# The weight stream of the first MoE layer, moved within its quarters

## The chip, the cores and the metric

One core of a Trainium2 chip. The metric is the device time of one execution in microseconds, as the median of several runs. Engines: PE (TensorE, with PEld for its weight loads), DVE (VectorE), ACT (ScalarE), POOL (GpSimd), SP (SyncE), which here only issues transfers.

## What is computed

A chain of three parts on 1152 tokens of width 512, in float32:

- attention over 2 x 8 heads of 1152 keys of width 64, the queries pooled by two (576 per head), with a softmax;
- MoE 1: `h = x @ w_in` (512 x 2048), `g = elu(h)`, that is h where it is positive and exp(min(h, 0)) - 1 elsewhere, then `g @ w_out` (2048 x 512);
- MoE 2: a normalisation by the root mean square over the width, `silu(xn @ w_gate) * (xn @ w_val)` (512 x 1536 each), then a product with `w_out` (1536 x 512).

## The kernel before

**Products.** Every matrix product runs on a high and a low part of both operands (xh, xl, wh, wl, in fp32r): for each block of 128 rows of depth three matmuls, high x high (L216), low activation x high weight (L217), high activation x low weight (L218). `product` (L211) writes one bank of 128 x 384 from four such blocks: 12 matmuls, a full product; with `ks` of two blocks, 6 matmuls, a half product. The tokens are three chunks c of 384. Seven PSUM banks are handed out in turn by `bank`.

**MoE 1** runs in four quarters q (L832). A quarter has four blocks of w_in (first products, each followed by an elu) and four of w_out (second products, summed into x2). Weights are numbered in that order, so that quarter q uses weights 8q to 8q+3 for its first products and 8q+4 to 8q+7 for its second; weight 31 is the last of MoE 1. In quarters 1 to 3 the first products of two chunks are computed for a pair of weights with seven products instead of eight (class `Elu`, one object a pair, steps m1 to m7; 8 and 9 are the plain products of the third chunk), from sums of weight parts (`combine`, four POOL steps sf, then `round`: a cast and a subtraction) and sums of x parts (`sums_from_x`, made once in quarter 0). `run` (L810) takes the steps in an order written out by hand. MoE 2 works the same way with `Gate` from its third pair on; its first two pairs are plain products (`unit`), of which the first needs weights 32 and 34, the next 33 and 35.

**Second products.** In quarters 0 to 2 (L859 to L872) the order is: blocks 0 and 1 of the depth for output m = 0, then for m = 1, then blocks 2 and 3 for both, then full products for m = 2 and 3, each over chunks 2, 0, 1. Quarter 3 (L873) goes chunk by chunk, so that the normalisation of a chunk (class `Norm`: `square`, `sums`, `spread`, `scale`) can begin while the next is computed; before it ACT loads the table for Sqrt (L874).

**Elu** (L236): ACT takes Relu(-h) (L243) and Exp of its negative (L244), DVE joins them (L245) two products later, and three products later ACT casts the high part (L246) and POOL subtracts for the low part (L64, tiles gl, gel). Of seven products of a pair, one (in `both`, with `into`) has its sum in SBUF rather than in a bank.

**The weight stream** (class `Stream`). The weights arrive as 64-bit numbers of 512 KB a block and are turned into float32 by a generator, one instruction a step: two ACT steps (we, wm: L120, L122), three DVE steps (L131, L133, L136; the last frees the raw tile, and the load of a later weight is issued on SP), an ACT cast to the high part (wh, L183) and a POOL subtraction for the low part (wl, L64). With a pair's sums come six further steps. Every product is followed by `ws.step(wi, k)`, which emits up to k steps behind it; all engines work in order of emission, so k sets where in each engine's queue the stream stands. `step` stops at two gates: eight weights may be held from weight wi on (wi is raised as weights are done with), and sums of a pair wait for `limit`:

```python
                if self.done == len(self.srcs) or (self.alloc and self.at >= (i + WB if len(self.pools) > 1 else NE)):
                    return
                if self.pair is not None and self.pair >= self.limit:
                    return
```

If a product asks for a weight that is not there, `get` emits the missing steps on the spot.

Of the kernel before, what the change touches and what calls it, by code (L numbers as in the profile page):

```python
# [11 lines left out]
AF = mybir.ActivationFunctionType  # L12
ALU = mybir.AluOpType
# [26 lines left out]
def tile_kernel(ctx: ExitStack, tc: tile.TileContext, qd, kd, vd, w1d, w2d, wgd, wvd, wod, rgd, outd):  # L40
    nc = tc.nc
    V, G, T, PE, SP = nc.vector, nc.gpsimd, nc.scalar, nc.tensor, nc.sync
# [20 lines left out]
    def lo_pool(o, i, h):  # L63
        G.tensor_tensor(out=o, in0=i, in1=f(h), op=ALU.subtract)  # L64
# [146 lines left out]
    def product(out, w, a, first, last, ks=range(4)):  # L211

        wh, wl = w
        for k in ks:
            ah, al = a(k)
            PE.matmul(out, lhsT=wh[:, k, :], rhs=ah, start=first and k == 0, stop=False)  # L216
            PE.matmul(out, lhsT=wh[:, k, :], rhs=al, start=False, stop=False)  # L217
            PE.matmul(out, lhsT=wl[:, k, :], rhs=ah, start=False, stop=last and k == 3)  # L218

    def xchunk(c):  # L220
        return lambda k: (xh[:, k, cs(c)], xl[:, k, cs(c)])
# [3 lines left out]
    def defer(n, work):  # L225
        pending.append([n, work])

    def flush():
        for item in pending:
            item[0] -= 1  # L230
        due = [work for n, work in pending if n == 0]
        pending[:] = [item for item in pending if item[0]]
        for work in due:
            work()

    def elu(v, gh, gl, add=None, into=None):  # L236

        e = gp.tile([128, CH], F32, tag="eg", name="eg", bufs=6)
        if add is not None:
            ps, v = v, v if into is None else into  # L240
            V.tensor_tensor(out=v, in0=ps, in1=add, op=ALU.add)
        flush()
        T.activation(out=e, in_=v, func=AF.Relu, scale=-1.0)  # L243
        T.activation(out=e, in_=e, func=AF.Exp, scale=-1.0)  # L244
        defer(2, lambda: V.scalar_tensor_tensor(out=e, in0=e, scalar=-1.0, in1=v, op0=ALU.add, op1=ALU.max))  # L245
        defer(3, lambda: (T.copy(gh, e), lo_pool(gl, e, gh)))  # L246

# [192 lines left out]
    def emit_x(p, xs, a=0, b=QS):  # L440
# [7 lines left out]
        else:  # L448
# [5 lines left out]
    wi = 0  # L454
    ge = tuple(gep.tile([128, NE, CH], F32R, name=f"ge{n}", tag=f"ge{n}") for n in "hl")
    ws = Stream([w for q in range(4) for w in w_in[4 * q:4 * q + 4] + w_out[4 * q:4 * q + 4]]
                + [w[2 * i + n] for i in range(6) for w in (wgd, wvd) for n in range(2)] + [wod[i] for i in range(12)])
# [211 lines left out]
    for n in range(NE):  # L669
        elu(fb[:, n, 0:CH], ge[0][:, n], ge[1][:, n])  # L670
        ws.step(0, 3)
# [5 lines left out]
    def bank():  # L677

        nonlocal nbank
        n, nbank = nbank % 7, nbank + 1  # L680
        if n == 4 and len(psb) == 1:
            with tc.using_default_side("right"):
                psb.append(ctx.enter_context(tc.tile_pool(name="psC", bufs=3, space=PSUM)))
        return psb[n >= 4].tile([128, 512], F32, tag="b", name="b", bufs=3 if n >= 4 else 4)[:, 0:CH]
# [3 lines left out]
    def g_block(c, k):  # L688

        n = 4 * c + k  # L690
        return [t[:, n] for t in ge] if n < NE else [t[:, n - NE] for t in g_at]
# [100 lines left out]
    class Elu(Branch):  # L792
# [10 lines left out]
        def out(self, k, c, p, add=None, into=None):  # L803
            elu(p, *g_block(c, self.k + k), add, into)
# [5 lines left out]
    def run(order, limit, k=1):  # L810
        ws.limit = limit
        for br, m in order:
            br.m(m)
            ws.step(wi, 3 * k if m > 7 else k)
# [3 lines left out]
    wi = 0  # L818
    for i in range(4):
        w = ws.get(i)  # L820
        for c in range(3):
            if c == 0 and i < NE:
                continue
            ps = bank()
            product(ps, w, xchunk(c), True, True)
            elu(ps, *g_block(c, i))
            ws.step(wi, 3)
            if i > 1 and c == 2:
                next(sums_of_x)
        wi += 1  # L830

    for q in range(4):  # L832
        if q:
            old, b = None, Elu(2 * q)
            run([(b, k) for k in (1, 6, 5, 8, 7, 2, 9)], 2 * q + 2)
            old, b = b, Elu(2 * q + 1)
            run([(b, 1), (old, 4), (b, 8), (old, 3)], 2 * q + 2)
            run([(b, k) for k in (6, 5, 2, 7, 9, 4, 3)], 2 * q + 3)
            ws.limit = 2 * q + 4
            wi += 4  # L840

        def out1(c, m, b, then=None, ks=range(4)):
            product(b, ws.get(8 * q + 4 + m), lambda k: g_block(c, k), True, True, ks)
            flush()
            if then:
                then()
            if ks[-1] < 3:
                return
            x = x2[:, m, cs(c)]
            if q:  # L850
                V.tensor_tensor(out=x, in0=b, in1=x, op=ALU.add)
                if q == 3:
                    norms[c].square(m)
            elif c == 1:
                V.tensor_copy(x, b)
            else:
                T.copy(x, b)

        if q < 3:  # L859
            banks = {}  # L860
            for m, ks in ((0, (0, 1)), (1, (0, 1)), (0, (2, 3)), (1, (2, 3)), (2, range(4)), (3, range(4))):
                for c in (2, 0, 1):
                    if (m, c) not in banks:
                        banks[m, c] = bank()
                    out1(c, m, banks[m, c], None, ks)
                    if q == 0 and (m, ks[0]) != (1, 2):
                        next(sums_of_x, None)
                        if m == 1:
                            next(sums_of_x, None)
                    ws.step(wi, 5 if len(ks) > 2 else 3 if ks[0] == 0 else 2)  # L870
                if ks[-1] == 3:
                    wi += 1  # L872
        else:  # L873
            T.activation(out=dummy, in_=eps, func=AF.Sqrt)  # L874
            for c in range(3):
                if c == 0:
                    bs = [bank() for n in range(4)]
                    for n in range(4):
                        out1(c, n, bs[n], None, (0, 1))
                        ws.step(wi, 2)  # L880
                for n in range(4):
                    if c:
                        out1(c, n, bank(), norms[c - 1].sums if n == 1 else None)
                    else:
                        out1(c, n, bs[n], None, (2, 3))
                    if c and n == 2:
                        norms[c - 1].spread()

                    if c and n == 4 - c:
                        norms[c - 1].scale()  # L890
                    ws.step(wi, ((3, 3, 3, 0), (3, 3, 3, 0), (0, 6, 3, 3))[c][n])
            wi += 4
# [101 lines left out]
    b = Gate(2)  # L994
    run([(b, 1), (b, 8), (b, 9), (b, 2)], 2, 4, 2)
    run([(b, 6), (b, 5)], 2, 4)
    old, b = b, Gate(3)
    run([(b, 1), (old, 7)], 2, 4)
    for n in range(3, 11):
        if n > 3:  # L1000
            old, b = b, Gate(n)
# [7 lines left out]
    b = Gate(11)  # L1009
# [87 lines left out]
```

## Time and profile before

| | us |
|---|---|
| three runs | 686.48, 686.5, 687.26 (median 686.5) |
| the profiled execution | 689.09 |
| its span, first to last instruction | 687.3 |

The granted TensorE clock is 0.989 of full speed in the mean over the span; 58.66 MB are read from HBM, 89 GB/s. The profile is one execution. Busy times are sums over all stages; how much a stage can give is read from the waits and the clock inside it. MoE 1 lies between about 245 and 459 us of the span, MoE 2 behind it.

### The profile page before, as it was taken

The numbers are of one execution on the slowest core, as the hardware profiler recorded it, in microseconds if no ns is written. First come the engines' busy times: TensorE is split into PE (matmuls) and PEld (weight loads), VectorE is DVE, ScalarE is ACT, GpSimd is POOL, SyncE is SP. The second block draws the span as 40 slices with busy tenths as digits, with TensorE's granted clock in tenths as the row PEclk, the third lists the DMA queues.
The fourth block names the chain that finished last, engine by engine and source line by source line (L and its number), as shares of the span: only waits on it lengthen the run. The fifth ranks groups of instructions, "written<-read, shape, count | busy, mean of one in ns | idle before, by whom it ended". The sixth has DMA issues, their size and how long they took to land.

```text
span 687.3 us, 11390 instructions
## 1 busy us (share of the span) xinstructions
PE 667.6 (97%) x4149; PEld 657.1 (96%) x4149; DVE 502.9 (73%) x870; ACT 471.3 (69%) x924; POOL 447.2 (65%) x406
## 2 busy tenths in 40 slices
PE   8999999999999999899999998898999999999997
PEld 7999999999999999899999997897989999999997
DVE  7989899998988978837766757487777876776300
ACT  6888889888988959758659569345667555645300
POOL 5999889888988207966757756363998965323300
PEclk9999999999999999999999999899999999999999
DMA  5523333223331003321221321101233322204200
GB/s 172 183 87 120 123 118 104 87 88 127 124 110 65 1 1 112 105 92 62 93 93 62 123 93 62 61 32 61 93 123 125 129 85 92 93 1 137 86 35 34
DMA packets 21624, 61.75 MB, mean 90 GB/s; under 512 B 2752, under 2 KB 5056, under 8 KB 21568
## 3 DMA queue, kind: packets, MB, share of 16 engines
q1 hardware_dynamic: 21568, 61.03, 26.6%
q8 instruction: 32, 0.52, 0.3%
q14 instruction: 24, 0.20, 0.1%
HBM read 58.66 MB, written 2.36 MB: 89 GB/s over the span
## 4 chain that ended last, share of the span: by engine, by line
PE 80%; ACT 6%; POOL 5%; DVE 5%; issue 1%; DMA 0%; DVEq 0%; ACTq 0%; SPq 0%; POOLq 0%
PE b L743 15%; PE s L346 12%; PE o L390 11%; PE b L218 10%; PE b L217 10%; PE b L216 10%; PE t L364 10%; POOL gl L64 2%; POOL wl L64 2%; ACT eg L243 1%; ACT xh L728 1%; ACT eg L244 1%; DVE x L940 1%; ACT wh L183 1%; DVE wt L136 1%
## 5 line engine op out<-in xcount | busy, mean ns | idle before, releaser
L64 POOL TENSOR_TENSOR wl<-wt,wh 128x512 fp32r<-128x512 f32 x68 | 91.3, 1342 | 86.7 <-ACT wh L183 81.1
L70 DVE TENSOR_TENSOR ptl<-t,pth 128x384 fp32r<-128x384 f32 x216 | 106.7, 549 | 5.3 <-ACT pth L372 4.7
L350 DVE TENSOR_SCALAR_CACHE_REDUCE p<-s 128x1152 f32<-128x1152 f32 x72 | 97.4, 1353 | 14.8 <-PE s L346 14.2
L372 ACT CAST pth<-t 128x384 fp32r<-128x384 f32 x216 | 89.2, 487 | 21.9 <-PE t L364 21.1
L346 PE MATMUL s<-kd,qt 128*128 128x384 f32 x480 | 98.8, 343 | 2.1 <-DVE p L350 2.0
L355 ACT ACTIVATE p<-p,st 128x1152 f32<-128x1152 f32 x72 | 91.5, 1271 | 1.2 <-DVE p L350 0.9
L216 PE MATMUL b<-xh,wh 128*128 128x384 f32 x260 | 88.3, 340 | 1.8 <-ACT wh L183 1.8
L218 PE MATMUL b<-xh,wl 128*128 128x384 f32 x260 | 88.1, 339 | 0.7 <-POOL wl L64 0.7
L217 PE MATMUL b<-xl,wh 128*128 128x384 f32 x260 | 88.0, 338 | 0.0
L346 PEld LDWEIGHTS s<-kd,qt 128*128 128x128 f32 x480 | 81.2, 189 | 5.5 <-DVE p L350 3.1
L390 PE MATMUL o<-pth,vd 128*128 128x256 f32 (+1 forms) x288 | 84.4, 315 | 0.0
L364 PE MATMUL t<-ident,p 128*128 128x128 f32 x648 | 82.5, 273 | 0.0
L390 PE MATMUL o<-ptl,vd 128*128 128x256 f32 (+1 forms) x288 | 78.5, 295 | 0.0
L364 PEld LDWEIGHTS t<-ident,p 128*128 128x128 f32 x648 | 75.0, 141 | 2.0 <-ACT p L355 0.3
L120 ACT ACTIVATE we<-wr 128x512 uint32<-128x512 uint32 x68 | 45.4, 668 | 39.1 <-DMA wr<-in_w_dram 17.1
L131 DVE TENSOR_SCALAR wm<-wm 128x512 f32<-128x512 f32 x63 | 43.7, 693 | 21.1 <-ACT wm L122 21.1
L122 ACT ACTIVATE wm<-wr 128x512 f32<-128x512 f32 x63 | 39.6, 629 | 25.3 <-DVE wt L136 25.1
L390 PEld LDWEIGHTS o<-pth,vd 128*128 128x128 f32 x288 | 54.4, 189 | 0.3
L390 PEld LDWEIGHTS o<-ptl,vd 128*128 128x128 f32 x288 | 54.4, 189 | 0.0
L64 POOL TENSOR_TENSOR gl<-eg,gh 128x384 fp32r<-128x384 f32 x36 | 39.1, 1103 | 18.8 <-ACT gh L246 18.7
L217 PE MATMUL b<-gl,wh 128*128 128x384 f32 x144 | 49.2, 342 | 2.1 <-POOL gl L64 2.0
L216 PEld LDWEIGHTS b<-xh,wh 128*128 128x128 f32 x260 | 49.2, 189 | 2.1 <-ACT wh L183 2.1
(195 smaller groups left out, 1771.8 us busy)
## 6 DMA issues: line engine op xcount, KB each, us to landing
wr<-in_w_dram SPq DMA_DIRECT2D x32, 512.0 KB, 3.2
rawq<-in_q_dram SPq DMA_DIRECT2D x15, 576.0 KB, 4.5
rawk<-in_k_dram SPq DMA_DIRECT2D x28, 288.0 KB, 2.8
wr<-in_wg_dram SPq DMA_DIRECT2D x12, 512.0 KB, 3.2
wr<-in_wv_dram SPq DMA_DIRECT2D x12, 512.0 KB, 3.2
wr<-in_wo_dram SPq DMA_DIRECT2D x12, 512.0 KB, 3.3
rawv<-in_v_dram SPq DMA_DIRECT2D x16, 288.0 KB, 2.8
out_dram<-o SPq DMA_DIRECT2D x12, 192.0 KB, 1.8
```

Of the source, the lines that this page charges most:

```text
L64: G.tensor_tensor(out=o, in0=i, in1=f(h), op=ALU.subtract)
L70: V.tensor_tensor(out=o, in0=i, in1=f(h), op=ALU.subtract)
L216: PE.matmul(out, lhsT=wh[:, k, :], rhs=ah, start=first and k == 0, stop=False)
L217: PE.matmul(out, lhsT=wh[:, k, :], rhs=al, start=False, stop=False)
L218: PE.matmul(out, lhsT=wl[:, k, :], rhs=ah, start=False, stop=last and k == 3)
L346: PE.matmul(s[:, m, 0:384], lhsT=a, rhs=b[:, 384 * m:384 * m + 384], start=n == 0, stop=n == len(parts) - 1)
L350: V.tensor_scalar(out=pt, in0=s[:, :, 0:384], scalar1=-0.0625, scalar2=None, op0=ALU.mult, op1=ALU.min, accum_out=st[p][:, 0, TILES[i][4], :])
L355: T.activation(out=pt, in_=pt, func=AF.Exp, scale=-1.0, bias=st[p][:, 0, TILES[i][4], :], accum_out=st[p][:, 1, TILES[i][4], :])
L364: PE.transpose(ps[:, k, :], src[:, 128 * b:128 * b + 128], ident)
L372: T.copy(oh, re(ps))
L390: PE.matmul(self.o[:, 0:self.N], lhsT=v[:, b, :], rhs=(pth, ptl)[u][:, g["buf"], b, g["c0"]:320], start=self.n == 0, stop=self.n == 17)
L743: PE.matmul(out, lhsT=a[x][:, k, :], rhs=b[y][:, k, :], start=first and (k, x, y) == (0, 0, 0), stop=last and (k, x, y) == (1, 1, 0), skip ...
```

## The change

- The first products of quarter 0 emit two stream steps instead of three behind those of weights 2 and 3.
- The second products of quarters 0 to 2 emit 0, 3, 4, 4, 7, 7 steps behind each product of their six groups, instead of 3, 3, 2, 2, 5, 5.
- In quarters 1 to 3, wi is raised by two when the first pair is done and by two more at the end, instead of by four at the end.
- The elu of a block whose sum is in SBUF takes min(h, 0) on DVE and Exp of it, instead of Relu(-h) on ACT and Exp of its negative.
- In quarter 0 the results of all three chunks are copied out by DVE, instead of two of them by ACT.
- The sums of x get two calls behind some products that had one.

```diff
         flush()
-        T.activation(out=e, in_=v, func=AF.Relu, scale=-1.0)
-        T.activation(out=e, in_=e, func=AF.Exp, scale=-1.0)
+        if into is not None:
+            V.tensor_scalar(out=e, in0=v, scalar1=0.0, scalar2=None, op0=ALU.min)
+        else:
+            T.activation(out=e, in_=v, func=AF.Relu, scale=-1.0)
+        T.activation(out=e, in_=e, func=AF.Exp, scale=-1.0 if into is None else 1.0)
...
             elu(ps, *g_block(c, i))
-            ws.step(wi, 3)
+            ws.step(wi, 3 if i < 2 else 2)
...
             run([(b, 1), (old, 4), (b, 8), (old, 3)], 2 * q + 2)
+            wi += 2
             run([(b, k) for k in (6, 5, 2, 7, 9, 4, 3)], 2 * q + 3)
             ws.limit = 2 * q + 4
-            wi += 4
+            wi += 2
...
-            elif c == 1:
+            else:
                 V.tensor_copy(x, b)
-            else:
-                T.copy(x, b)
...
                     if q == 0 and (m, ks[0]) != (1, 2):
                         next(sums_of_x, None)
-                        if m == 1:
+                        if (m, ks[0]) != (0, 0):
                             next(sums_of_x, None)
-                    ws.step(wi, 5 if len(ks) > 2 else 3 if ks[0] == 0 else 2)
+                    ws.step(wi, 7 if len(ks) > 2 else 4 if ks[0] else 3 * m)
```

## Rows read from the trace of the kernel before

**Rows 1.** The page, part 1: busy us, share of the span, instructions.

```profile
PE 667.6 (97%) x4149; PEld 657.1 (96%) x4149; DVE 502.9 (73%) x870; ACT 471.3 (69%) x924; POOL 447.2 (65%) x406
```

**Rows 2.** Waits of PE: engine, line, releaser: us in total, times, longest.

```profile
PE b L216 <- ACT wh L183: 5.3, 2, 3.5
PE b L218 <- POOL wl L64: 2.8, 2, 2.1
...
PE b L217 <- POOL gl L64: 2.0, 1, 2.0
```

**Rows 3.** Stretches of 5 us: busy us (instructions) by engine, granted clock, DMA share, GB/s.

```profile
275.00:280.00 5.00, 5.00 (x31) 5.00 (x30) 4.97 (x6) 4.13 (x8) 5.00 (x5) 1.00 0.09 34
285.00:290.00 5.00, 5.00 (x25) 5.00 (x25) 2.28 (x4) 2.90 (x8) 4.46 (x3) 0.81 0.45 151
315.00:320.00 5.00, 5.00 (x31) 5.00 (x30) 2.84 (x6) 4.91 (x12) 5.00 (x5) 1.00 0.20 79
500.00:505.00 5.00, 3.71 (x21) 3.22 (x20) 3.21 (x7) 4.10 (x9) 5.00 (x4) 1.00 0.31 108
```

**Rows 4.** Timeline of POOL around 273 to 283 us: start, length, operation.

```profile
273.56 4.41 POOL L64 TENSOR_TENSOR gl<-eg,gh 128x384 fp32r<-128x384 f32 x3
277.92 2.03 POOL L64 TENSOR_TENSOR wl<-wt,wh 128x512 fp32r<-128x512 f32 x1
279.90 2.70 POOL L64 TENSOR_TENSOR gl<-eg,gh 128x384 fp32r<-128x384 f32 x2
```

**Rows 5.** Timeline of PE around 280 us: start, length, operation.

```profile
279.28 0.33 PE L216 MATMUL b<-gh,wh 128*128 128x384 f32 x1
...
280.32 0.34 PE L216 MATMUL b<-gh,wh 128*128 128x384 f32 x1
...
286.93 0.34 PE L217 MATMUL b<-gl,wh 128*128 128x384 f32 x1
```

**Rows 6.** Timeline of PE around 426 to 437 us.

```profile
426.02 0.33 PE L218 MATMUL b<-geh,wl 128*128 128x384 f32 x1
...
437.20 0.34 PE L217 MATMUL b<-gl,wh 128*128 128x384 f32 x1
```

**Rows 7.** Timeline of ACT around 426 to 430 us.

```profile
425.89 1.28 ACT L874 ACT_TABLE_LOAD   x1
...
427.29 0.49 ACT L246 CAST gh<-eg 128x384 fp32r<-128x384 f32 x1
...
428.80 0.49 ACT L246 CAST gh<-eg 128x384 fp32r<-128x384 f32 x1
429.20 0.61 ACT L183 CAST wh<-wt 128x512 fp32r<-128x512 f32 x1
```

**Rows 8.** Timeline of POOL around 429 to 433 us.

```profile
429.38 1.96 POOL L64 TENSOR_TENSOR gl<-eg,gh 128x384 fp32r<-128x384 f32 x2 [0.51 <-ACT gh L246]
431.29 1.27 POOL L64 TENSOR_TENSOR wl<-wt,wh 128x512 fp32r<-128x512 f32 x1
```

**Rows 9.** Timeline of PE around 466 to 478 us.

```profile
466.08 0.83 PE L711 MATMUL b<-ones,sq 128*128 128x1 f32 x6 [0.74 <-DVE sq L706]
...
470.84 0.34 PE L218 MATMUL b<-xh,wl 128*128 128x384 f32 x1
...
477.47 0.79 PE L721 MATMUL b<-ident,rr 128*128 128x128 f32 x3
```

**Rows 10.** Timeline of DVE around 462 to 472 us.

```profile
462.13 0.69 DVE L131 TENSOR_SCALAR wm<-wm 128x512 f32<-128x512 f32 x1
...
465.94 5.62 DVE L940 TENSOR_TENSOR x<-x 128x768 f32<-128x768 f32 x4
```

**Rows 11.** The page, part 6: DMA issues, KB each, us from issue to landing.

```profile
wr<-in_w_dram SPq DMA_DIRECT2D x32, 512.0 KB, 3.2
```

**Rows 12.** Timeline of ACT around 354 us.

```profile
353.83 0.47 ACT L755 COPY m<-b 128x384 f32<-128x384 f32 x1
```

**Rows 13.** The chain that ended last, in order of time: start, length, what.

```profile
351.23 3.15 PE b L743 x18
```

## The prediction

> **What bounds the kernel now.** I read the page first. TensorE (PE) is busy for 97% of the span [rows 1], so this change can give back only what PE loses by waiting and by running slowly after a wait. The list of waits by engine says where: the longest are for a weight's high part from ACT and its low part from POOL, and one of 2.0 us for the low part of an activation [rows 2]. The stretches of 5 us place them. Between the listed places PE is busy throughout; ACT is the fullest helper in the first products of a quarter (4.91 of 5 us), without holding PE up [rows 3]. After each long wait the granted clock falls: 0.81 over the 5 us behind the 2.0 us wait [rows 3]. So a wait costs its length and slow matmuls behind it. Quarters 1 and 2 can hardly gain; what can are four places: the start of quarter 0's second products, the start of quarter 3's, the change from MoE 1 to MoE 2, and the first combined products of MoE 2.
>
> **What moves.** I counted on the code which stream step is emitted behind which product. Second products of quarters 0 to 2: before 3x(3+3+2+2+5+5) = 60 steps each, after 3x(0+3+4+4+7+7) = 75; none behind the first three half products, more behind the full ones. Quarter 0's first products with weights 2 and 3 lose five steps in all. The first products' own 26 steps stay, but the stream may now take the buffers of a pair two weights earlier. By the count, the low part of weight 31 (last of MoE 1) is emitted in quarter 3's first products, before it was behind the third half product of its second ones; weight 35's (the last that MoE 2's first units need) moves from behind MoE 2's first unit into quarter 3. Every weight carries the same steps as before: 5 on ACT and DVE, a cast, a POOL subtraction, one DMA on SP's queue. None is added; each load is still issued when DVE has released its buffer, and SP has no other transfer queued in this part. The extra calls for the sums of x in quarter 0 change nothing: ten are left, and the tenth is reached behind the same product.
>
> **Place A, second products of quarter 0.** POOL runs three activation subtractions in 4.41 us, weight 6's in 2.03, two more in 2.70, and the last of these is what PE waits for [rows 4]. At full speed a matmul starts every 0.173 us (six between 279.28 and 280.32); from 280.32 to 286.93 are 16, 2.8 us of work in 6.6, so 3.8 us are lost [rows 5]: 2.0 in the wait [rows 2], 1.8 to the slow clock behind it. The change emits weight 6's subtraction five products later. Its 2.03 us come off POOL ahead of the last one, which then ends by 280.57, against 280.49 when PE asks. ACT and DVE lose at least three and one stream steps there, so its inputs come sooner too. I take 3.8; the low end is 2.0, POOL's own time alone, with the slow clock kept.
>
> **Place B, second products of quarter 3.** From 426.19 (the end of 426.02's slot) to 437.20 PE issues 16 matmuls, 2.8 us of work in 11.0: 8.2 us lost, to weight 31 and the slow clock after it [rows 6]. Afterwards weight 31 is ready. What is late next? The activation of this half product's last block. ACT first loads the Sqrt table (425.89), casts one block at 427.29, and casts the needed one at 428.80 [rows 7]. In the new order weight 33's cast (0.53, from 429.20 to 429.73) stands between, instead of two steps of weight 32, so the needed cast ends near 428.6. POOL takes one subtraction to about 428.9, weight 33's (1.27) to 430.1, then the needed one (0.98) to 431.1 [rows 8]. PE asks at 426.19 + 10 x 0.173 = 427.9. That leaves 3.2 us, and as in A 1.8 of slow clock: 5.0 instead of 8.2. I take 3.2. The ends are 0 (another wait as long) and 8.2 (none).
>
> **Place C, change to MoE 2.** From 470.84 to 477.47 PE makes 13 steps, 2.3 us in 6.6: 4.4 lost to weight 35 and the clock; the sum of squares waits another 0.7 [rows 9]. Weight 35's cast sat behind casts that wait for DVE's four subtractions (5.62 us from 465.94), and these sat behind three stream steps from 462.13 on, 0.69 each [rows 10]. The gate of eight weights keeps the stream out of the last third of quarter 3's products, so these 2.1 us leave DVE's queue, and weight 35 is ready long before. I take 4.4 + 0.7 = 5.1. The low end is 2.5, the two waits for weight 35 alone (5.3 - 3.5 and 2.8 - 2.1 [rows 2]), with a slow clock kept behind another wait: the scale of the last third, late for a PE that arrives sooner.
>
> **Place D, first combined products of MoE 2.** PE idles 1.29 of 5 us at 500 [rows 3]. The stream is a step or two further by emission order, but PE arrives some 5 us sooner after the change of MoE. I take half, 0.6, between 1.3 and a loss of 1.
>
> **The moved steps.** Six Relu steps leave ACT, each near its 0.49 us step of [rows 7], and six minimum steps join DVE. No row shows one; the ends are nothing and 0.69 us, the 128x512 step of [rows 10], and with POOL in its way 0.69 + 1.47 = 2.2: POOL's 128x384 subtraction takes 1.47 us (4.41/3) while DVE is busy 4.97 of 5 us [rows 3, 4], but 0.98 at another place [rows 8]. The Exp behind each now waits for DVE, and behind that Exp on ACT stand the Relu and casts of the next blocks. I take nothing for all six: their results are needed only in the next half products, and ACT, the fuller engine, loses more than it waits [rows 3]. Without that cover they cost up to 6 x 2.2 = 13 us. The Trainium skill (SBUF — State Buffer, section "Who interferes with whom") speaks against such a move: tensor_scalar between SBUF tiles can enter a two-port mode, in which DVE and GpSimd exclude each other for a whole instruction. By that rule each step would stand behind a POOL subtraction or hold one up; the two POOL durations above agree with it, and the sum would be near 0 instead of 12.7 only if all six reached PE.
>
> The eight result copies of quarter 0 that move from ACT to DVE cost under 0.69 each beside products of 2.1 us, and seven banks rotate; I cost them at nothing. If DVE were late with one, PE would wait for its bank.
>
> **New pressure.** Seven steps behind a 2.1 us product is a weight per 2.7 us. With two raw buffers two weights need: a load 3.2 [rows 11], two ACT steps near 0.53 each [rows 7], three DVE steps of 0.69 [rows 10]: 6.3, so 3.2 for each, and with queueing some 3.3. The stream therefore falls behind, and at the end of quarter 1's second products ACT reaches the next copy late. Before, that copy ran at 353.83, although its product ended near 351.23 + 3.15/3 + 0.2 = 352.5 [rows 12, 13]. Carried forward weight by weight I get about 354.7, then two DVE steps to 356.0; PE needs them at 351.23 + 3.15 + 2.1 = 356.5 [rows 13]. I cost this at nothing; the cover is half a microsecond thick in quarter 1, one in quarter 0. If it goes, a start costs up to 2 us and 1.8 of slow clock.
>
> **Sum.** 3.8 + 3.2 + 5.1 + 0.6 = 12.7 us. The profiled execution took 689.09 with a span of 687.3, 1.8 us around it; it should go to 676.4 with a span of 674.6. The median of the runs is 686.5, 2.6 below the profiled one: 673.8. About 0.2% (1.4 us) is what a measurement here tells from no change.
>
> **Rivals.** (1) Place B vanishes whole, if ACT's queue is clear and the needed subtraction slips ahead: 5.0 more, 668.8. For it speaks that ACT has fewer steps in quarter 3; against it that the table load and the chain in front of it don't move [rows 7]. Chance 0.12. (2) The wait changes place: quarters 1 to 3 each start with a stall of up to 2 us plus slow clock, together 3 to 10 us: 677 to 684. For it speaks the half microsecond of cover; against it that in the first products the stream stands still at its gate more often, which leaves ACT room. 0.20. (3) The stream does not get ahead, because gate or raw buffers stop it: only A is gained, 682.7. For it: one more buffer gate hit in quarter 2's last two products by the count. 0.07. (4) Slower: ACT is held by late loads at all three starts, past the 356.5 of [rows 13]. It decides from 12.7/3 = 4.2 us a start, so 2.4 of stall and 1.8 of clock; that is ACT some 3 us later than I carried it, near 358. At 3.5 of stall each: 686.5 - 12.7 + 3 x 5.3 = 689.7. 0.04. (5) DVE's minimum steps and POOL's subtractions exclude each other, and all six reach PE at their full bound of 13 us: 686.8, no change. Against it: no listed wait of PE is for such a step [rows 2]. 0.02. That is the rule of the Trainium skill named above, taken to its end.
>
> **Numbers.** The forecast, 0.55, spans 670 to 677. The range takes in rival 1, most of rival 2 and the ends of B and C: 668.0 to 681.0, leaving out rivals 3 to 5 and the end of 2, about 0.2. Faster by over 0.2%: 0.55 + 0.12 + 0.20 + 0.07 = 0.94; same 0.02; slower 0.04.
>
> **What would show it.** Right: no wait of PE for a low activation part near 280, no clock under full there; no wait for a weight's parts at quarter 3's start, instead one near 3 us for an activation's low part; none for weight 35; first products of quarters 1 to 3 without PE waits. Wrong: PE waiting for a copy's reader or a bank at those starts, ACT's raw weight step waiting longer for loads and PE behind it, or a weight still the releaser at quarter 3.

## The result and the profile after

The changed kernel took 679.56 us (median of four runs, 679.0 to 680.05), the kernel before 686.88 beside it (four runs, 686.48 to 689.01): a ratio of 0.9887, interval 0.9865 to 0.9909. Measured again (e8, below) the ratio was 0.9881 (0.9863 to 0.9899). So it is faster, by 7.3 us and not by the 12.7 of the sum; the time lies inside the range of 668 to 681, near its slow end, and outside the forecast's 670 to 677. The profiled execution took 680.05 with a span of 678.2.

Part 1 of the page of the changed kernel, busy us by engine; it answers to [rows 1]:

```profile
PE 663.7 (98%) x4149; PEld 654.5 (96%) x4149; DVE 511.3 (75%) x884; ACT 465.2 (69%) x910; POOL 446.0 (66%) x406
```

PE's busy time fell by 3.9 us with the same 4149 matmuls: I read that as fewer slow matmuls; the waits that went come on top. DVE has 14 instructions more and ACT 14 fewer: six minimum steps and eight copies.

The waits of PE in the changed kernel (engine, line, releaser: us in total, times, longest), which answer to [rows 2]:

```profile
PE b L217 <- POOL gl L64: 2.5, 2, 1.9
PE b L746 <- DVE u L781: 2.1, 1, 2.1
...
PE b L216 <- ACT gh L249: 1.4, 1, 1.4
...
PE b L746 <- POOL tsl L64: 0.7, 1, 0.7
```

No weight is waited for any more: 5.3 and 2.8 us of [rows 2] are gone. In their place stand an activation's high and low part, and a wait of 2.1 us for DVE's `u` (L781: the sum that DVE reads off step m6's bank; step m7 goes on in that bank and waits for it) that the kernel before had nowhere at this length. The stretches place them (columns: stretch, length, busy us and instructions of PE, PEld, DVE, ACT, POOL, granted clock, DMA share, GB/s); they answer to [rows 3]:

```profile
285.00:290.00 5.00, 5.00 (x31) 5.00 (x30) 4.47 (x8) 2.22 (x4) 3.44 (x4) 1.00 0.59 195
300.00:305.00 5.00, 4.29 (x25) 3.97 (x24) 3.95 (x6) 2.44 (x5) 4.92 (x6) 1.00 0.51 187
305.00:310.00 5.00, 2.94 (x17) 2.62 (x16) 2.04 (x4) 3.96 (x7) 4.46 (x5) 1.00 0.30 106
...
430.00:435.00 5.00, 3.63 (x11) 3.63 (x12) 1.22 (x3) 1.58 (x4) 3.16 (x4) 0.50 0.26 97
```

Behind place A the clock is full now (1.00 where it was 0.81). The new hole is at 305 to 310, where quarter 1's first pair begins, and place B still loses clock (0.50).

**Where the time went, place by place.** The start of one and the same matmul in two profiles tells how far ahead the changed kernel is there. Taken against a second execution of the kernel before (experiment e0, span 684.6), in us:

| the matmul stands | before, again | after | ahead of before |
|---|---|---|---|
| last of the attention | 239.81 | 240.38 | -0.57 |
| in place A, past the wait | 281.90 | 281.13 | 0.77 |
| quarter 1, step m7, past the wait for u | 305.38 | 307.81 | -2.43 |
| quarter 3's second products, past place B | 436.15 | 436.66 | -0.51 |
| MoE 2, past place C | 474.60 | 469.60 | 5.00 |
| MoE 2, first combined products (D) | 501.24 | 494.77 | 6.47 |

The differences between successive rows are the gains: A 1.3, start of quarter 1 -3.2, the stretch to the end of place B 1.9 (of it 1.6 at B), C 5.5, D 1.5; together 7.0, near the medians' 7.3, after 0.6 lost ahead of the change. Against the profile that the prediction read (span 687.3), with A taken behind its slow matmuls, the same list is A 2.9, start of quarter 1 -3.2, B 2.4, C 5.2, D 1.6.

**The new wait.** The timeline of ACT in the changed kernel (start, length, operation; in brackets idle time and releaser):

```profile
302.98 0.60 ACT L183 CAST wh<-wt 128x512 fp32r<-128x512 f32 x1
305.74 1.04 ACT L170 CAST tsh<-sf 128x1024 fp32r<-128x1024 f32 x1 [2.16 <-POOL sf L162]
306.69 0.47 ACT L758 COPY m<-b 128x384 f32<-128x384 f32 x1
```

of POOL:

```profile
299.17 2.38 POOL L64 TENSOR_TENSOR tsl<-sf,tsh 128x1024 fp32r<-128x1024 f32 x1
301.51 1.29 POOL L64 TENSOR_TENSOR wl<-wt,wh 128x512 fp32r<-128x512 f32 x1
302.76 0.74 POOL L156 TENSOR_TENSOR sf<-wt 128x256 f32<-128x256 f32 x1
...
304.96 0.74 POOL L162 TENSOR_TENSOR sf<-wt,sf 128x256 f32<-128x256 f32 x1
305.66 1.27 POOL L64 TENSOR_TENSOR wl<-wt,wh 128x512 fp32r<-128x512 f32 x1
```

and of PE:

```profile
307.81 0.45 PE L746 MATMUL b<-tsh 128*128 128x384 f32 x1 [2.06 <-DVE u L781]
```

The copy of m1 (L758) could run by 303 us (in e4, below, it does at 302.83), but it stands on ACT behind the cast of a pair's sums (L170), which is emitted by the stream behind the last second product. That cast waits 2.16 us for POOL, and POOL is the late one: a pair of weights costs it two subtractions of 1.3, four sums of 0.74 and one subtraction of 2.38, some 7.9 us, and from 293.7 on one follows the other. That run itself began late: POOL stood idle for 2.98 us before it, until a cast of ACT whose raw weight ACT had awaited for 2.56 us (to 291.94). So the load, which the prediction did count, has a share in it. Copy 306.69, DVE's u 307.19, PE 307.81: one chain.

### The profile page after: what moved, and what is told of

Its sections match the earlier page's. It is cut to its first block, busy times and chain, and to the rows that moved or that the text cites. A ratio compares the mean times of both kernels' runs of the same rounds, so it can differ in the third digit from the quotient of the medians.

```text
span 678.2 us, 11378 instructions
## 1 busy us (share of the span) xinstructions
PE 663.7 (98%) x4149; PEld 654.5 (96%) x4149; DVE 511.3 (75%) x884; ACT 465.2 (69%) x910; POOL 446.0 (66%) x406
## 4 chain that ended last, share of the span: by engine, by line
PE 47%; POOL 4%; ACT 2%; DVE 2%; issue 1%; DMA 1%; DVEq 0%; ACTq 0%; POOLq 0%; SPq 0%
PE b L746 15%; PE b L217 11%; PE b L216 11%; PE b L218 10%; POOL wl L64 1%; POOL tsl L64 1%; DMA wr<-in_w_dram 1%; POOL gl L64 0%; POOL sf L162 0%; POOL sf L158 0%; POOL sf L156 0%; ACT xh L731 0%; POOL xl L64 0%; ACT we L120 0%; ACT wm L122 0%
## 5 line engine op out<-in xcount | busy, mean ns | idle before, releaser
L70 DVE TENSOR_TENSOR ptl<-t,pth 128x384 fp32r<-128x384 f32 x216 | 106.7, 549 | 4.9 <-ACT pth L375 4.4
L216 PE MATMUL b<-gh,wh 128*128 128x384 f32 x144 | 49.0, 341 | 1.4 <-ACT gh L249 1.4
```

What stands on the lines that cost most here:

```text
L70: V.tensor_tensor(out=o, in0=i, in1=f(h), op=ALU.subtract)
```

## Experiments

The theory: the 3 us at quarter 1's start are lost because the stream's cast waits for POOL with the copy of m1 queued behind it; the rest of the error is the size of the slow clock at A and B. Rivals: the copies moved to DVE, the moved Relu steps, or the stream's pace as such, which would give a wait back elsewhere. Ratios are to the kernel before, run beside each on the same chip.

**e0: the kernel before once more.**

> The kernel before once more, for a second profile. Its first profile gives 9.0 us to the change (offsets of the same matmuls), the medians only 7.3. If the first profile was a long execution, this one's span is nearer to 684.7 (median 686.5 less 1.8 around the span), and one of the places A to D loses less than 3.8, 8.2, 5.1 and 1.3 us, most likely by a shorter stretch at the lower clock. If instead the profile itself lengthens the kernel, the span is 687 again and the places lose the same.

It took 686.4, span 684.6, against 689.09 and 687.3 of the profile that was read. The waits are the same, `gl` too. Its stretch behind place A:

```profile
285.00:290.00 5.00, 5.00 (x30) 5.00 (x29) 3.69 (x7) 3.07 (x8) 5.00 (x5) 1.00 0.49 164
```

and its wait there:

```profile
PE b L217 <- POOL gl L64: 2.0, 1, 2.0
```

The same wait of 2.0 us, and a clock of 1.00 where [rows 3] has 0.81. Of the two profiled executions only the first has the slow clock at A; by the starts of the same matmuls it cost 1.6 us there, most of the 2.6 by which that execution stood above the median.

**e1: three steps instead of seven behind the last second product of quarter 0**, so that the pair's cast is emitted behind the copy.

```diff
-                    ws.step(wi, 7 if len(ks) > 2 else 4 if ks[0] else 3 * m)
+                    ws.step(wi, 3 if (q, m, c) == (0, 3, 1) else 7 if len(ks) > 2 else 4 if ks[0] else 3 * m)
```

> The changed kernel, with three stream steps instead of seven behind the very last second product of quarter 0, so that the cast of pair 3's sums is emitted behind the copy of quarter 1's first product and not ahead of it. Theory (queue on ACT behind POOL): PE waited 2.06 us at 307.8 because that copy stood on ACT behind the cast, which waited for POOL's fourth sum step. That wait goes, the copy runs near 303.5, the 0.70 us wait at 301.6 stays: 679.6 - 2.1 = 677.5. Rival (the copies moved to DVE make DVE late): DVE has the same work, the wait stays, 679.6. Rival (late loads set the pace): the wait shrinks by less than 0.5 us, above 679.0.

678.2 us, ratio 0.9862 (0.9836 to 0.9887). ACT at quarter 1's start, with the cast behind the copy:

```profile
302.93 0.47 ACT L758 COPY m<-b 128x384 f32<-128x384 f32 x1
305.19 1.05 ACT L170 CAST tsh<-sf 128x1024 fp32r<-128x1024 f32 x1 [1.78 <-POOL sf L162]
```

ACT at quarter 3's start, the copy behind a late load:

```profile
401.85 0.66 ACT L120 ACTIVATE we<-wr 128x512 uint32<-128x512 uint32 x1 [3.39 <-DMA wr<-in_wg_dram]
...
402.96 0.48 ACT L758 COPY m<-b 128x384 f32<-128x384 f32 x1
```

The cast still waits for POOL, but nothing hangs on it: PE no longer waits at quarter 1's start. It waits 1.1 us at quarter 2's and 0.8 at quarter 3's instead, where ACT's first steps of a weight stand ahead of the copy and wait for a load (2.41 us at 352.22, and the row above). So the theory holds at the first place, and much of what it returns is given back at the other two as long as their order stays: the time alone does not tell e1 (expected at 677.5) from the changed kernel.

**e4: no steps behind the last second product of quarters 0 to 2**, seven steps later, behind m5 of the next quarter.

```diff
-            run([(b, k) for k in (1, 6, 5, 8, 7, 2, 9)], 2 * q + 2)
+            run([(b, k) for k in (1, 6, 5)], 2 * q + 2)
+            ws.step(wi, 7)
+            run([(b, k) for k in (8, 7, 2, 9)], 2 * q + 2)
...
-                    ws.step(wi, 7 if len(ks) > 2 else 4 if ks[0] else 3 * m)
+                    ws.step(wi, 0 if (m, c) == (3, 1) else 7 if len(ks) > 2 else 4 if ks[0] else 3 * m)
```

> The changed kernel with no stream step behind the last second product of quarters 0 to 2, and seven steps more behind the third combined product (m5) of the next quarter. Copies of a quarter's first product then stand ahead of the stream's steps in ACT's queue. Theory (the copy waits in ACT's queue behind a stream step that itself waits, for POOL in one quarter, for a load in another): no PE wait for the sum u at any quarter's start, neither at 307.8 (2.06 us in the changed kernel) nor at quarters 2 and 3, where the kernel with three steps got waits of 1.1 and 0.8; the 0.7 us wait at 301.6 stays: 679.6 - 2.1 = 677.5 and a profiled span near 676.1. Rival (the stream's own pace by loads is the bound, so what one quarter gains the next gives back): PE waits for a weight or a sum of weights in quarter 2 or 3 instead, 679 or more.

676.75 us, ratio 0.9834 (0.981 to 0.9858), below the interval of the changed kernel. Its waits of PE; no u of L781 is among them:

```profile
PE b L217 <- POOL gl L64: 2.6, 2, 1.9
...
PE b L216 <- ACT gh L249: 1.4, 1, 1.4
...
PE b L746 <- POOL tsl L64: 0.9, 1, 0.9
```

and ACT at quarter 1's start:

```profile
302.83 0.47 ACT L758 COPY m<-b 128x384 f32<-128x384 f32 x1
303.20 0.61 ACT L183 CAST wh<-wt 128x512 fp32r<-128x512 f32 x1
305.49 1.05 ACT L170 CAST tsh<-sf 128x1024 fp32r<-128x1024 f32 x1 [1.68 <-POOL sf L162]
```

Same weights, same steps, same late cast (305.49 against 305.74): only what is queued behind it differs, and PE waits for u at none of the three starts (the 0.9 for a pair's low part, at 301.36, stays). About 3.2 us (0.9881 - 0.9834 = 0.0047, of 687) come back: the wait for u with its restart, 2.3, and an excess that is inside the spread of the runs. That the stream's pace must give the wait back elsewhere falls.

**e6: two of three copies of quarter 0 back on ACT**, in one execution.

```diff
-            else:
+            elif c == 1:
                 V.tensor_copy(x, b)
+            else:
+                T.copy(x, b)
```

> The changed kernel with two of three result copies of quarter 0 back on ACT. Theory (their engine does not matter): PE's wait for u at 307.8 stays within 0.7 us of 2.06, since the cast ahead of the copy still waits for POOL; span within 1 us of 678.2. Rival (eight copies on DVE made DVE late): that wait goes, span near 676. A third possibility: ACT, waiting for products in order, starts raw weights later and the wait grows by 1 us or more.

679.35 us, as the changed kernel. PE waits for u as before:

```profile
PE b L746 <- DVE u L781: 2.3, 2, 2.1
```

The moved copies neither make nor cure the wait. That rival falls.

**e7 and e9: all Relu steps back on ACT**, in one execution (e7) and in six (e9).

```diff
-        if into is not None:
-            V.tensor_scalar(out=e, in0=v, scalar1=0.0, scalar2=None, op0=ALU.min)
-        else:
-            T.activation(out=e, in_=v, func=AF.Relu, scale=-1.0)
-        T.activation(out=e, in_=e, func=AF.Exp, scale=-1.0 if into is None else 1.0)
+        T.activation(out=e, in_=v, func=AF.Relu, scale=-1.0)
+        T.activation(out=e, in_=e, func=AF.Exp, scale=-1.0)
```

> The changed kernel with all Relu on ACT again. Theory (the six moved steps are hidden): the waits of PE are the same ones within 0.3 us each, span within 0.7 us of 678.2. Rival (DVE's minimum and POOL's subtraction exclude each other and delay blocks): a wait of PE gets shorter and the span falls by 1 us or more. Other rival (ACT needed the relief): new waits in the first products of quarters 1 to 3, span over 679.5.

> The changed kernel with all Relu on ACT again, now timed. Its one look gave 676.58, but its profile had no slow stretch behind quarter 3's start. Theory (the six moved steps are hidden, and that look was a lucky execution): median within 0.7 us of the changed kernel's beside it. Rival (the moved steps cost 2 to 3 us): median under 677.5 while the changed kernel stays at 679.

e7 took 676.58, which looks like 3 us of gain; but its wait for u is the same 2.1 us, and six runs of e9 gave 680.0 (677.12 to 681.84), ratio 0.9883 (0.9859 to 0.9906), against 0.9881 of the changed kernel beside it. So the time shows no cost of the moved steps. One wait does: PE waits 1.06 us for gh at B in e7 and in e9, against 1.38 in the changed kernel and 1.35 in e8. What e7 had was clock; the stretch behind place B in e7, then in e9, where PE's waits at B are the same within 0.01 us:

```profile
430.00:435.00 5.00, 4.88 (x28) 4.88 (x29) 3.62 (x7) 1.57 (x4) 3.30 (x4) 1.00 0.06 25
...
430.00:435.00 5.00, 4.91 (x15) 4.91 (x16) 2.42 (x4) 1.55 (x3) 3.02 (x4) 0.50 0.05 20
```

**e8: the changed kernel again, beside e9 to e11.**

> The changed kernel once more, timed beside the next three. Theory (behind a wait of PE of 2 us or more the clock sometimes falls and sometimes not, in executions of one kernel): median 679.3 within 0.7, the same waits of PE within 0.2 us each (2.1 for the sum u, 1.4 and 1.9 at quarter 3's start), and behind quarter 3's start a slow stretch that may differ from the 2.6 us lost in its first profile, anywhere from 0 to 2.6. Rival (the clock's fall is fixed by the order of the work): the same slow stretch again.

679.27 us (678.83 to 681.33), ratio 0.9881. The waits are those of the first profile: 2.1 for u, 1.3 for gh, 1.9 for the longest gl. Its stretch behind place B:

```profile
430.00:435.00 5.00, 3.98 (x15) 3.98 (x16) 2.40 (x4) 1.68 (x4) 3.56 (x5) 0.71 0.22 88
```

After the same waits within 0.03 us the clock is 0.71 here and 0.50 in the first profile of this kernel.

**e2: quarter 3's steps behind its first four half products 0, 4, 2, 2 instead of 2 each**, so that weight 33 comes behind the activation that place B waits for.

```diff
-                        ws.step(wi, 2)
+                        ws.step(wi, (0, 4, 2, 2)[n])
```

> The changed kernel, with 0, 4, 2, 2 stream steps instead of 2, 2, 2, 2 behind the first four half products of quarter 3's second products, so that weight 33's cast and subtraction are emitted behind the activation's. Theory (weight 33 stands in the way): the needed cast comes 0.5 us sooner and the needed subtraction 1.3 sooner than 430.33; PE's waits of 1.38 and 1.89 become about 0.9 and 1.1: 678.3, and down to 676 if the shorter wait keeps the clock up. Rival (the Sqrt table and the chain ahead of it set the end): the waits change by under 0.3 us, 679.6.

677.62 us, ratio 0.9854 (0.9832 to 0.9876), an interval that overlaps the changed kernel's. Its waits of PE:

```profile
PE b L746 <- DVE u L781: 2.0, 1, 2.0
PE b L217 <- POOL gl L64: 1.9, 2, 1.2
...
PE b L216 <- ACT gh L249: 0.9, 1, 0.9
```

Place B's two waits fall from 3.3 to 2.1 (0.9 + 1.2), and POOL now takes weight 33's subtraction behind the needed one. But the stretch behind the wait for u reads, in this execution,

```profile
305.00:310.00 5.00, 3.45 (x13) 3.45 (x14) 2.44 (x5) 3.45 (x7) 4.30 (x3) 0.76 0.29 105
310.00:315.00 5.00, 5.00 (x27) 5.00 (x27) 3.65 (x8) 4.21 (x10) 1.43 (x2) 0.90 0.21 51
```

where the changed kernel had 1.00 behind a wait as long. By the starts of the same matmuls that is 1.5 us.

**e3: wi raised by four at the end of a quarter, as before**, all else changed.

```diff
-            wi += 2
...
-            wi += 2
+            wi += 4
```

> The changed kernel, with the pair's buffers given back as before (wi raised by four at the end). By the count of steps the stream then stands at its gate for most of quarter 2's second pair, weight 31 is still ready in quarter 3's first products, weight 33 is cast behind the activation casts of quarter 3's start, and weight 35 with three DVE steps of weight 36 falls into the last third of quarter 3. Theory (giving back is worth its place in C alone): no wait for a weight comes back; place B loses some 1.3 us less, place C some 2 us more: 680.3, between 679 and 681.5. Rival (giving back is what frees weight 31): a wait for weight 31 of 3 us or more is back, 683 or more.

681.93 us, ratio 0.9907 (0.9876 to 0.9939): above the 679 to 681.5 expected, and with an interval that overlaps the changed kernel's. Its waits of PE:

```profile
PE b L746 <- DVE u L781: 3.6, 3, 2.1
...
PE b L216 <- ACT gh L249: 0.2, 1, 0.2
```

and ACT at quarter 2's start:

```profile
354.40 0.66 ACT L120 ACTIVATE we<-wr 128x512 uint32<-128x512 uint32 x1 [2.40 <-DMA wr<-in_w_dram]
...
356.04 0.47 ACT L758 COPY m<-b 128x384 f32<-128x384 f32 x1
```

With the gate raised late the stream stands at other steps when the quarters start: all three wait, which was not expected, the copy at quarter 2 comes at 356.04 instead of 354.39, and place B's wait for gh shrinks from 1.4 to 0.2. At place C new waits stand, as expected: 1.1 us for a step of ACT (L932) and 0.3 for a sum of squares. No weight is late even so.

**e11: the kernel before with the new steps of the second products alone** (0, 3, 4, 4, 7, 7).

```diff
-                    ws.step(wi, 5 if len(ks) > 2 else 3 if ks[0] == 0 else 2)
+                    ws.step(wi, 7 if len(ks) > 2 else 4 if ks[0] else 3 * m)
```

> The kernel before with one part of the change alone: 0, 3, 4, 4, 7, 7 stream steps behind the second products of quarters 0 to 2. By the count the gate of eight weights stops the stream for most of quarter 2's second pair, weights 31 and 35 are still ready before they are asked for, weight 35 and three DVE steps fall into the last third of quarter 3. Theory: this part carries nearly all of the gain, no wait for a weight is left, and it comes out like the changed kernel without the early giving back (681.9): 682, between 680 and 683.5; the wait for u at quarter 1's start is there, 2 us or more. Rival (the other parts carry a good share): a wait of PE for weight 31 or 35 stays, 684 or more.

681.31 us, ratio 0.9921 (0.9894 to 0.9948), 2.0 above the changed kernel beside it. Its longest wait of PE:

```profile
PE b L743 <- DVE u L778: 4.8, 3, 2.2
```

The new counts alone bring the weights in time (no wh or wl is waited for) and 6.1 of the 8.1 us (687.41 against 681.31 and 679.27). They also bring the wait for u, at all three starts, 4.8 in all. In the changed kernel it is 2.1 at one start, so the gate raised in two parts, as e3 shows too, is what keeps two starts free. e11 has e3's waits of 1.1 and 0.3 at place C as well.

**e5 and e10: the repairs together.** e5 is e4 with ten steps behind m5 and 4, 4, 2 steps behind the last but one second product of quarters 0, 1, 2; with e2's counts; and with two stream steps of quarter 0 moved from its last first products to earlier ones (3, 3, 2, 1, 1 instead of 2 each), ahead of place A. e10 also takes e7's edit.

```diff
-            ws.step(wi, 3 if i < 2 else 2)
+            ws.step(wi, 3 if i < 3 else 2 - (c > 0))
...
+            ws.step(wi, 10)
...
-                    ws.step(wi, 7 if len(ks) > 2 else 4 if ks[0] else 3 * m)
+                    ws.step(wi, 0 if (m, c) == (3, 1) else (4, 4, 2)[q] if (m, c) == (3, 0) else 7 if len(ks) > 2 else 4 if ks[0] else 3 * m)
...
-                        ws.step(wi, 2)
+                        ws.step(wi, (0, 4, 2, 2)[n])
```

> The idea of the kernel before this one, with four steps instead of seven (two in quarter 2) behind the last but one product too and ten more behind m5, with 0, 4, 2, 2 steps at quarter 3's start, and with weight 5's cast and subtraction one product earlier in quarter 0 (3, 3, 2, 1, 1 steps behind the first products of weights 2 and 3, ten as before). Theory: 2.1 us of the wait for u, 1.3 or more at quarter 3's start, 0.6 at the start of quarter 0's second products: 675.5, between 674 and 677. Rival (each gain is given back by the next wait): no better than 677.5.

> The best kernel so far (675.17) with all Relu on ACT again. Theory (hidden): 675.2 within 0.8. Rival (the moved steps cost): 673 or less.

e5: 675.17 us, ratio 0.9813 (0.9793 to 0.9834); e10: 674.32, ratio 0.9806 (0.9786 to 0.9825), not told apart from e5. Both beat the kernel before and the changed kernel. The waits of PE in e5:

```profile
PE b L217 <- POOL gl L64: 1.9, 2, 1.2
...
PE b L216 <- ACT gh L249: 0.8, 1, 0.8
PE b L746 <- POOL tsl L64: 0.7, 1, 0.7
```

No u of L781, and the mean clock of the span is 1.000. So with the starts cleared and quarter 3's order changed as well, 12.2 and 13.1 us are gained, about the prediction's sum. The third repair did nothing: at place A PE waits 0.75 us in e5, where the changed kernel waits 0.64 and the expectation had 0.6 to gain.

## Why the prediction was right and wrong

**Right: what the change does.** Every wait for a weight is gone, and places A to D are where time came back. **Place C** was put at 5.1 and gave 5.5. **Place B**'s next wait was named (the activation of the half product's last block, behind the Sqrt table and weight 33) and sized at 3.2 us; it is 1.38 for the high part and 1.89 for the low one. ACT in the changed kernel there:

```profile
426.16 1.28 ACT L876 ACT_TABLE_LOAD   x1
...
427.96 0.61 ACT L183 CAST wh<-wt 128x512 fp32r<-128x512 f32 x1
428.48 0.92 ACT L249 CAST gh<-eg 128x384 fp32r<-128x384 f32 x2
```

POOL there, where the needed subtraction is the first of the two at 430.33 and ends near 431.3, estimated 431.1:

```profile
429.09 1.28 POOL L64 TENSOR_TENSOR wl<-wt,wh 128x512 fp32r<-128x512 f32 x1
430.33 1.95 POOL L64 TENSOR_TENSOR gl<-eg,gh 128x384 fp32r<-128x384 f32 x2
```

**The moved steps and the copies**, costed at nothing: right for the copies (e6), and for the steps as far as the time can tell (e9). The reason given, that ACT loses more than it waits, did not hold: six Relu steps are 2.9 us (6 x 0.49), and ACT waited 9.3 us for the six minimum steps, part of which it would have waited for `u` as well (1.18 us at the sixth in e9). The sixth reaches PE. This step in the changed kernel, and the Exp behind it:

```profile
419.99 0.84 DVE L244 TENSOR_SCALAR eg<-u 128x384 f32<-128x384 f32 x1
...
420.87 0.53 ACT L247 ACTIVATE eg<-eg 128x384 f32<-128x384 f32 x1 [2.07 <-DVE eg L244]
```

From there ACT works without a pause to the cast that PE waits for at B. Where this step takes 0.81 to 0.84 us (here, e8, e4), PE waits 1.35 to 1.38 for gh; where it takes 0.36 (e1) or is not there (e7, e9), 1.03 to 1.06. So its price is 0.3 us.

**Wrong, the largest term: "New pressure", costed at nothing.** The start of quarter 1 lost 3.2 us (2.3 for u and 0.9 behind a wait for a pair's low part, which in e8 was 0.2). The bound in the prediction was made of a load, ACT steps and DVE steps, 6.3 us for two weights; POOL's 7.9 us for the same two weights, the longest of the four, was left out, and with it the cast that waits for POOL at the head of ACT's queue. The cover named there ("one" us at the end of quarter 0) was worth nothing because of it.

At the other start that the text carried forward, the copy was put at 354.7, ran at 354.39, and PE did not wait. That is in part luck: the text held PE's time there at that of the kernel before, although its own place A should bring PE 3.8 us sooner. In the changed kernel the loss at quarter 1's start used up what A gave, so that PE came to this place at 356.11, against 356.32 before. In e1, with quarter 1's start cleared, PE comes 2.9 us sooner and the copy only 1.1 sooner (353.33), and PE waits 1.1. So rival 2, priced at 677 to 684, came true at one of its three places; e1, e3 and e11 show how near the other two were. That the measured time lies in rival 2's range is luck in part too: the starts cost 3.2 us, and the mis-sized terms for A and B the rest.

**Wrong: the slow clock at A, 1.8 of its 3.8 us.** e0 shows the same 2.0 us wait without it. It was also counted twice: the term took it out of the profiled execution, and the step from that execution to the median took off 2.6 us, most of which was this slow clock. Nor is the wait gone whole; POOL there in the changed kernel:

```profile
273.50 1.54 POOL L64 TENSOR_TENSOR wl<-wt,wh 128x512 fp32r<-128x512 f32 x1 [0.44 <-ACT wh L183]
274.99 6.08 POOL L64 TENSOR_TENSOR gl<-eg,gh 128x384 fp32r<-128x384 f32 x4
```

Weight 6's subtraction left the stretch, as said, but weight 5's, one product later than before, came into it, and the last subtraction ends at 281.07 instead of 280.57: PE waits 0.64. Weight 5's is not what makes it late, though: e5 takes it ahead of the stretch again, and its five activation subtractions from 273.59 on take 7.77 us, where [rows 4] have 7.11 for five. In the changed kernel four of the 36 subtractions gl take 1.73 to 1.75 us, all beside DVE's 128x768 subtractions for the sums of x (L661, L70), and the other 32 near 1.0; three of the four slow ones are in this stretch, and in e5 four. That the sums of x hold POOL up here is read from this, and no run moved them. The gain at A was 1.3 against a like execution.

**Wrong in size: B and D.** B kept its waits as predicted, but the slow matmuls and the restart behind them took 2.9 us in that execution instead of 1.8 (from 427.50 to 436.86 PE makes 18 steps, 3.1 us of work: 6.2 lost, 3.3 of it waits). Its gain was 1.6, not 3.2; how much of B's loss is clock differs by execution (e7 and e9). D gave 1.5 instead of 0.6, since a wait for a pair's low part (0.6 in e0) went there too.

In numbers, against the second profile of before: 12.7 less 3.2 (new pressure), 2.5 (A) and 1.6 (B), plus 0.4 (C), 0.9 (D) and 0.3 (between quarter 1's start and B) is 7.0 us.

## What to carry to other kernels

When a background stream is made to run earlier, add up its work on every engine, also on the one that no list of waits names, and ask at each stage's start what of the critical path is queued behind a step of the stream that waits; where a step is emitted counts beside how many are (e4 moves seven of them and gains what the wait cost). If the same change also brings the bottleneck engine to a later place sooner, hold the stream against that sooner time. Before a slow clock in a profile becomes a term of a sum, look at a second execution, and never take the same microseconds off once as a term and once as the way to the median.

## What the runs showed of the hardware

**A slow clock behind a wait of 2 to 3 us is a matter of the execution.** One wait of 2.0 us at A: 0.81 granted in one execution of the kernel before, 1.00 in the next. One of 2.0 to 2.1 us for u: 1.00 in the changed kernel, 0.76 in e2. Place B with waits of 3.0 us in all, in e7 and e9, which are one kernel: 1.00 and 0.50 over the same five microseconds. By the starts of the same matmuls the three are worth 1.6, 1.5 and 2.5 us. This fits the spread of the runs of one kernel: in e9 the fastest run (677.12) had a mean granted clock of 1.000, the slowest (681.84) 0.992. What decides it was not found.

**DVE's minimum step depends on POOL.** In the changed kernel, beside POOL's subtraction from 309.81 to 311.10:

```profile
310.35 0.96 DVE L244 TENSOR_SCALAR eg<-u 128x384 f32<-128x384 f32 x1
```

In e1, with POOL idle:

```profile
407.24 0.36 DVE L244 TENSOR_SCALAR eg<-u 128x384 f32<-128x384 f32 x1
```

Of the six in the changed kernel two, with POOL idle, take 0.36 us; the four that meet a POOL subtraction take 0.84 to 1.20, and each ends 0.2 us behind that subtraction's end. The Trainium skill (SBUF — State Buffer, section "Who interferes with whom") says that a tensor_scalar between SBUF tiles can enter a two-port mode, in which it and a GpSimd instruction exclude each other for the whole instruction; these rows agree with it. Here it costs the 0.3 us at place B, at the one step of the six with no slack behind it on ACT.
